# Two small transposes and a run of zero matmuls change places ahead of the first weight group

## Chip, cores, metric

One core of a Trainium2 chip. By the record the rounds of e1 to e4 ran on chip 0, those of e5 to e8 on chip 4 and those of e9 to e12 on chip 12, so a run is compared with the kernel before of its own rounds. Times are device microseconds (us) of that core; lower is better. A span in the trace counts from the first recorded instruction and is some 1.9 us shorter than the reported time.

## The reference, cut to what matters

```python
# [cut: inputs; x is 2048 x 576, weights 576 x 4608, all bf16]
xn = layernorm(x)
return x + ssm(xn, Lambda_re, Lambda_im, log_dt, ...) + glu(xn, w_gate, w_up, w_down)

def glu(x, w_gate, w_up, w_down):
    return (sigmoid(x @ w_gate) * (x @ w_up)) @ w_down
```

The gated part dominates on TensorE. The state-space part needs three rows of 576 constants (log_dt, Lambda_re, Lambda_im), spread over partitions.

## The kernel before

At the start, x tiles of 128 rows are normalised, transposed on TensorE into a PSUM tile, and copied to SBUF by ACT and DVE. Two x tiles make the first 256 columns of xT, which the first weight group multiplies. The three constant rows are loaded as 27 rows of 64 (`crows`) and turned by two small transposes, written into a spare tenth block of the *second* x tile's PSUM tile.

```python
def consts_transpose(ps):                       # two transposes, 27 x 64 each
    for half in (slice(0, H), slice(H, P)):
        nc.tensor.transpose(ps[half, 0:3 * NH], crows[:], ident[0:3 * NH, 0:3 * NH])

def busy(n, cols):                              # zero matmuls: nobody reads the result
    for i in range(n):
        nc.tensor.matmul(start_groups[0].ps[:, i % 2, 0:cols], warm[:, 0:P], warm[:, 0:cols], ...)

ptrs = [psum.tile([P, NH + 1, P], BF16, ...) for _ in range(2)]   # NH = 9 blocks and a spare
busy(10, TB)                                    # at the very start, while x is loaded
busy(6, P)
# [cut]
for tt in range(2):
    ln_recip(0, tt, tt + 1)
    ln_norm(tt, twice=False)
    start_transpose(tt)                         # 18 transposes into ptrs[tt]
consts_transpose(ptrs[1][:, NH, :])             # the spare block of the SECOND x tile
busy(18, P)
start_copy(0, slice(0, NH), nc.scalar.copy)     # ACT: all 9 blocks of the first x tile
ln_stats(2)
start_copy(1, slice(0, 5), nc.scalar.copy)      # ACT: blocks 0 to 4 of the second
# [cut]
start_copy(1, slice(5, NH), nc.vector.tensor_copy)   # DVE: blocks 5 to 8 of the second
for tt in range(2, TT_B):
    ln_recip(0, tt, tt + 1)
    ln_norm(tt, twice=False)
start_groups[0].mms(slice(0, 2 * P))            # the first weight group (L501)
start_transpose(2)
start_transpose(3)
start_groups[1].mms(slice(0, 2 * P))            # the second weight group
# [cut]
consts_copy(ptrs[1][:, NH, :])                  # DVE reads the constants, some 4 us later
```

The kernel states no waits: the framework sets semaphores from what each instruction reads and writes. GpSimd loads the weights, one transfer of 288 KB for each half (gate on partitions 0 to 63, up on 64 to 127).

Of the kernel before, what the change touches and what calls it, by code (L numbers as in the profile page):

```python
# [66 lines left out]
def kernel(  # L67
# [18 lines left out]
    P = 128  # L86
# [107 lines left out]
    def consts_transpose(ps):  # L194
        for half in (slice(0, H), slice(H, P)):
            nc.tensor.transpose(ps[half, 0:3 * NH], crows[:], ident[0:3 * NH, 0:3 * NH])  # L196
# [40 lines left out]
    def ln_recip(nb, t0, t1):  # L237
        nc.vector.reciprocal(rstds[nb][:, t0:t1], rstds[nb][:, t0:t1])
# [4 lines left out]
    def ln_norm(tt, twice=True):  # L243

        nb, tl = divmod(tt, TT_B)
        m, r = mvs[nb][:, tl, 0:1], rstds[nb][:, tl:tl + 1]
        if twice:
            xn = xn_bufs[ln_count[0] % XN_BUFS]
            ln_count[0] += 1
            nc.vector.tensor_scalar(xn[:], halves2(xts[tt][:]), m, r, ALU.subtract, ALU.mult)  # L250
            xns[tt] = xn[:, :, 0, :]
            xn2[tt] = xn
        else:
            xn = hpool.tile([P, NH, H], BF16, name="xn0", tag="hst", bufs=10)
            nc.vector.tensor_scalar(xn[:], xts[tt][:].rearrange("p (c h) -> p c h", h=H), m, r,
                                    ALU.subtract, ALU.mult)
            xns[tt] = xn[:]
# [479 lines left out]
    def busy(n, cols):  # L737
        for i in range(n):
            nc.tensor.matmul(start_groups[0].ps[:, i % 2, 0:cols], warm[:, 0:P], warm[:, 0:cols], start=True, stop=True)  # L739
# [4 lines left out]
    def start_transpose(tt):  # L744
        for c in range(NH):
            for half in (slice(0, H), slice(H, P)):
                nc.tensor.transpose(ptrs[tt % 2][half, c, :], xns[tt][:, c, :], ident[:])  # L747

    def start_copy(tt, cs, eng):
        eng(xT_tile(0)[:, cs, tt * P:(tt + 1) * P], ptrs[tt % 2][:, cs, :])  # L750
# [4 lines left out]
    for tt in range(2):  # L755
        ln_recip(0, tt, tt + 1)
        ln_norm(tt, twice=False)
        start_transpose(tt)
    consts_transpose(ptrs[1][:, NH, :])
    busy(18, P)  # L760
    start_copy(0, slice(0, NH), nc.scalar.copy)
    ln_stats(2)
    start_copy(1, slice(0, 5), nc.scalar.copy)
# [128 lines left out]
```

## Time and profile before

| kernel before | value |
|---|---|
| time, 3 runs | 507.41 us median (507.36 to 507.81) |
| profiled run | 507.63 us, span 505.7 |
| TensorE busy | 500.9 us (99%) |
| last of the three constants' rows, issue to landing | 2.41 to 7.66 |
| first weight group starts | 9.04 |
| second weight group starts | 11.25 |

A timeline row gives start, duration, engine, source line, operation, output and inputs, and a count where equal rows are merged; in brackets stands how long the engine was idle before it and what ended that. PE is TensorE, PEld its weight load, ACT is ScalarE, DVE is VectorE and POOL is GpSimd; xT is the transposed x, pgu a group's output in PSUM. L196 are the constants' transposes, L739 the zero matmuls, L747 the x transposes, L750 the copies out of PSUM, L501 a weight group, L255 the normalisation of an x tile. Where I give a landing or a signal, it is from the trace's semaphore records, which hold the time of every increment. Lines that do not bear on the point are left out of the views without a mark.

### The profile page before, as it was taken

Reading aid. Unit: us, or ns where it says so; the run is one execution under the profiler, and the core shown is the slowest. Engines: PE = TensorE matmul, PEld = TensorE weight load, DVE = VectorE, ACT = ScalarE, POOL = GpSimd, SP = SyncE. Lnnn points to the kernel's source line nnn. Section 1 sums busy time; section 2 is a strip of 40 time slices with the busy share of each in tenths; the row PEclk is TensorE's granted clock in tenths of the full one; section 3 lists DMA queues with packets and bytes.
Section 4 is the critical chain, followed back from the end, with each engine's and each line's share of the span. In section 5 each row is a group of like instructions: output and inputs, shape, how many; then the busy total and the mean of one; then the engine's idle time right before and its main releaser. Section 6 shows DMA issues by size and latency. Waiting matters only on the chain.

```text
span 505.7 us, 10662 instructions
## 1 busy us (share of the span) xinstructions
PE 500.9 (99%) x4536; PEld 289.6 (57%) x4536; DVE 324.6 (64%) x706; ACT 204.8 (40%) x368; POOL 90.8 (18%) x134
## 2 busy tenths in 40 slices
PE   8999999999999999999999999999999999999997
PEld 5544675444477444467764444774444774446775
DVE  5889797887888687878687768786675222222111
ACT  4955733556500756530016655005655005553000
POOL 7216320123100043110001231100431001300000
PEclk9999999999999999999999999999999999999999
DMA  8997595055220096241340652200643201600101
GB/s 207 205 183 232 134 204 89 19 147 141 49 49 25 1 180 152 68 119 58 83 95 6 160 141 49 47 25 1 162 106 86 48 25 27 184 1 1 36 25 35
DMA packets 40949, 45.59 MB, mean 90 GB/s; under 512 B 28614, under 2 KB 32326, under 8 KB 40902
## 3 DMA queue, kind: packets, MB, share of 16 engines
q0 software_dynamic: 10608, 34.22, 28.1%
q1 hardware_dynamic: 29862, 10.37, 10.6%
q8 instruction: 35, 0.57, 0.5%
q10 hardware_dynamic: 432, 0.33, 0.2%
q14 instruction: 12, 0.10, 0.1%
HBM read 34.36 MB, written 2.36 MB: 73 GB/s over the span
## 4 chain that ended last, share of the span: by engine, by line
PE 98%; DMA 1%; SPq 0%; issue 0%; DVE 0%
PE pgu L501 55%; PE pd L575 34%; PE pbu L530 7%; DMA crows<-in_A_Lambda_im_dram 1%; PE pd L583 1%; PE ptr L747 0%; PE pgu L739 0%; SPq L139 0%; SPq L192 0%; DVE ob L584 0%; PE ptr L196 0%
## 5 line engine op out<-in xcount | busy, mean ns | idle before, releaser
L501 PE MATMUL pgu<-xT,wgu 64*128 64x512 bf16 (+1 forms) x2628 | 283.7, 373 | 0.0
L501 PEld LDWEIGHTS <-wgu 64*128 64x128 bf16 x2628 | 127.7, 94 | 150.9 <-issue 0.5
L575 PE MATMUL pd<-wd,hT 128*128 128x288 bf16 x1128 | 141.4, 286 | 0.0
L507 ACT ACTIVATE sT<-pgu 128x512 bf16<-128x512 f32 x144 | 86.4, 600 | 120.8 <-PE pgu L501 119.8
L575 PEld LDWEIGHTS <-hT 128*128 128x128 bf16 x1128 | 109.9, 98 | 30.1 <-DVE hT L510 0.8
L510 DVE TENSOR_TENSOR hT<-sT,uT 128x512 bf16<-128x512 bf16 x144 | 60.6, 421 | 94.8 <-ACT uT L508 94.5
L508 ACT CAST uT<-pgu 128x512 bf16<-128x512 f32 x144 | 84.0, 583 | 0.0
L154 POOL DMA_DIRECT2D wgu<-in_B_w_gate_dram x36 | 27.6, 766 | 234.9 <-PE pgu L501 222.8
L536 ACT COPY bure<-pbu 128x512 f32<-128x512 f32 x16 | 9.4, 585 | 88.8 <-PE pbu L530 75.0
L160 POOL DMA_DIRECT2D wd<-in_B_w_down_dram x36 | 26.3, 734 | 98.6 <-PE pd L575 98.5
L595 DVE TENSOR_TENSOR acc<-acc,pd 128x576 f32<-128x576 f32 x32 | 24.0, 750 | 27.7 <-PE pd L575 27.7
L592 DVE TENSOR_TENSOR ob<-acc,pd 128x576 bf16<-128x576 f32 x15 | 11.3, 754 | 40.9 <-PE pd L575 40.9
L530 PE MATMUL pbu<-xT,bt 64*128 64x512 bf16 x288 | 33.7, 376 | 0.0
L575 PEld LDWEIGHTS <-hst 128*128 128x128 bf16 x270 | 26.4, 98 | 6.7
L154 POOL DMA_DIRECT2D wgu<-in_B_w_up_dram x36 | 26.5, 736 | 1.9 <-DMA wgu<-in_B_w_up_dram 1.9
L445 DVE TENSOR_TENSOR_SCAN gre<-r,g0re,wrim 128x512 bf16<-128x512 f32 x20 | 25.6, 1278 | 0.1
L575 PE MATMUL pd<-ctre,hst 128*128 128x288 bf16 x120 | 24.6, 286 | 0.0
L575 PE MATMUL pd<-ctim,hst 128*128 128x288 bf16 x120 | 24.6, 286 | 0.0
L530 PEld LDWEIGHTS <-bt 64*128 64x128 bf16 x288 | 13.8, 94 | 17.1 <-issue 0.7
L452 DVE TENSOR_TENSOR_SCAN gim<-r,g0im,wrim 128x512 bf16<-128x512 f32 x16 | 20.4, 1274 | 0.0
L230 DVE BATCH_NORM_STATS2 bnst<-xt 128x6 f32<-128x288 bf16 x32 | 12.5, 432 | 2.3 <-DMA xt<-in_A_x_dram 2.2
L431 DVE TENSOR_TENSOR wrim<-T,bure 128x512 bf16<-128x512 bf16 x20 | 13.7, 684 | 0.0
(119 smaller groups left out, 279.6 us busy)
## 6 DMA issues: line engine op xcount, KB each, us to landing
wgu<-in_B_w_gate_dram POOLq DMA_DIRECT2D x36, 288.0 KB, 4.2
wgu<-in_B_w_up_dram POOLq DMA_DIRECT2D x36, 288.0 KB, 4.8
wd<-in_B_w_down_dram POOLq DMA_DIRECT2D x36, 288.0 KB, 5.6
out_dram<-ob SPq DMA_DIRECT2D x15, 144.0 KB, 1.8
xt<-in_A_x_dram SPq DMA_DIRECT2D x10, 144.0 KB, 2.7
xt<-in_A_x_dram POOLq DMA_DIRECT2D x4, 144.0 KB, 7.5
bt<-ctre POOLq DMA_DIRECT2D x2, 288.0 KB, 6.4
bt<-ctim POOLq DMA_DIRECT2D x2, 288.0 KB, 7.8
```

Source lines behind the costliest of these rows:

```text
L154: eng.dma_start(w[rows, :, :], src[:, fs].rearrange("(c p) f -> p c f", p=H))
L160: nc.gpsimd.dma_start(wd[:], B_w_down[f0:f0 + FP * P, :].rearrange("(n p) d -> p n d", p=P))
L431: nc.vector.tensor_mul(w, t1, a[:])
L445: nc.vector.tensor_tensor_scan(gre[:], r_bc, w[:, 0, :], g0re[:, col], ALU.mult, ALU.add)
L452: nc.vector.tensor_tensor_scan(gim[:], r_bc, w[:, 1, :], g0im[:, col], ALU.mult, ALU.add)
L501: nc.tensor.matmul(self.ps[:, gi, cols], w[rows, c, fs], xT[self.nb][rows, c, cols], start=c == 0, stop=c == NH - 1)
L507: nc.scalar.activation(sT[:], self.ps[:, 0, :], ACT.Sigmoid)
L508: nc.scalar.copy(uT[:], self.ps[:, 1, :])
L510: nc.vector.tensor_mul(h[:], sT[:], uT[:])
L530: nc.tensor.matmul(out, w, xT[self.nb][rows, c, ts_], start=c == 0, stop=c == NH - 1)
L575: nc.tensor.matmul(out, lhsT, rhs[:, a * DH:(a + 1) * DH], start=i == 0, stop=i == n - 1)
L595: nc.vector.tensor_add(halves(acc[:]), halves(acc[:]), pd[:, :, 0:DH])
```

## The change

Its intent: TensorE stood still until the constants' rows had landed. With the zero matmuls first, the rows have time to land behind them; and since TensorE then waits less, 14 zeros are to do where 18 stood.

```diff
         ln_norm(tt, twice=False)
         start_transpose(tt)
+    busy(14, P)
     consts_transpose(ptrs[1][:, NH, :])
-    busy(18, P)
     start_copy(0, slice(0, NH), nc.scalar.copy)
```

## The prediction

> **What bounds the kernel now.** I first read the page's engine shares and its chain of work that ended last, to see whether anything but TensorE sets the time.
>
> ```profile
> PE 500.9 (99%) x4536; PEld 289.6 (57%) x4536; DVE 324.6 (64%) x706; ACT 204.8 (40%) x368; POOL 90.8 (18%) x134
> PE 98%; DMA 1%; SPq 0%; issue 0%; DVE 0%
> ```
>
> TensorE is the bound from the first real weight group to the end; DMA is 1% of the chain. So whatever moves the start of that group (L501) moves the end by as much, and nothing else at the start counts. Next I read the chain in order of time over the first 60 us:
>
> ```profile
> 2.41 5.25 DMA crows<-in_A_Lambda_im_dram
> 7.66 0.14 issue
> 7.79 0.20 PE ptr L196 x2
> 7.99 1.11 PE pgu L739 x18
> 9.11 1.09 PE pgu L501 x18
> 10.19 1.13 PE ptr L747 x36
> 11.32 45.79 PE pgu L501 x450
> ```
>
> The constants' rows (crows) land at 7.66; only then can their two transposes (L196) run, then 18 zero matmuls (L739), then the first weight group. TensorE had finished the transposes of the second x tile by about 7.03: the timeline of that stretch starts the last of them at 6.97, and they are spaced 0.056 a pair. It therefore stands idle from 7.03 to 7.76, behind a transfer whose result is not needed until 12.52 (the casts to cvals). That wait is what the change aims at. Then I read the timeline between 6 and 9.3 us, all engines, for what else the first group needs:
>
> ```profile
> 6.70 1.12 ACT L750 COPY xT<-ptr 128x1152 bf16<-128x1152 bf16 x1 [0.95 <-PE ptr L747]
> 7.76 0.14 PEld L196 LDWEIGHTS <-crows 27*64 27x64 bf16 x2 [0.73 <-issue]
> 7.79 0.20 PE L196 MATMUL ptr<-ident,crows 27*64 27x27 bf16 x2 [0.60 <-DMA crows<-in_A_Lambda_im_dram]
> 7.92 1.01 PEld L739 LDWEIGHTS <-warm 128*128 128x128 bf16 x18
> 8.03 0.69 ACT L750 COPY xT<-ptr 128x640 bf16<-128x640 bf16 x1 [0.22 <-PE ptr L196]
> 8.76 0.42 DVE L750 COPY xT<-ptr 128x512 bf16<-128x512 bf16 x1 [0.41 <-ACT xT L750]
> 9.04 1.16 PE L501 MATMUL pgu<-xT,wgu 64*128 64x256 bf16 x18
> ```
>
> The line to dwell on is the ACT copy at 8.03. It moves the first five column blocks of the second x tile out of PSUM, and the first weight group reads them. ACT ended its earlier copy at 7.82, and the x transposes were long done, but it waited 0.22 more for L196: the constants are written into the same PSUM tile as that x tile. The semaphore records agree: TensorE's completion count moves at 6.67 (first x tile) and next at 8.01 (constants), never at the end of the second x tile. The copy signals at 8.73, so it is already done when the first group starts at 9.04. The second half of the weights, one transfer of 288 KB issued at 2.33, lands at 8.46 by its semaphore.
>
> **What the Trainium skill says.** "PSUM — Partial Sum Buffer", under the bank collisions, asks that accesses be guarded by bank and quadrant. A block here is 256 bytes and a bank is 2 KiB by that page, so blocks 0 to 4 lie in the tile's first bank and the constants, in block 9, in its second: the copy need not wait. The trace shows that this program's dependency is coarser; it waits. "TensorEngine Tiling (Array Packing)", Key Properties, says a change of tiling mode drains TensorE. The trace agrees: where 64-row groups give way to transposes, nine pairs of 0.109 from 9.04 end at 10.02, yet the next row starts at 10.12, so a switch costs about 0.09. "TensorE: Matmul & The Clock Gate", in "What's actually happening", says the array halves its clock after an idle window of about 3.4 us. The zero matmuls are there for that: the first ten took 0.43 each for 512 columns, those at 7.93 are spaced 0.056 for 128. No run here shows how long an idle is too long, but the present 0.73 did not slow the matmuls after it.
>
> **The change, part by part.** *Moved:* 14 zero matmuls now stand directly behind the second x tile, where nothing holds them. They start at 7.03 + 0.09 (switch) = 7.12, and take about 14 x 0.056 + 0.01 = 0.80, to 7.92. The old wait for the transfer is thereby covered: crows landed at 7.66. *Removed:* four zero matmuls, 4 x 0.056 = 0.22. *The constants* come after a switch, weight load at 7.92 + 0.10 = 8.02, matmul 0.03 later at 8.05. In the kernel before, the completion count moved 0.21 after the second matmul started (7.80 to 8.01), so now at 8.26, against 8.01.
>
> Taken alone, TensorE's own stream would reach the weight group at about 8.05 + 0.13 = 8.18, or 0.86 earlier than 9.04. But the group needs two more things. Weights: landed at 8.46, plus the 0.10 that crows took from landing to weight load, 8.56. Copy: it still waits for the constants, now behind the zeros, so it starts at 8.26 + 0.02 = 8.28, signals 0.70 later (8.03 to 8.73 before) at 8.98, and TensorE sees it some 0.04 later (the x tile signalled at 5.92 was loaded at 5.96): **9.02**. The maximum is 9.02, against 9.04. The saving is about 0.02 us: the visible wait is removed and comes back as an idle of some 0.8 us between the constants and the first group.
>
> Behind that: the DVE copy of the remaining blocks and the normalisation of x tiles 2 and 3 move with the ACT copy, 0.25 later. Block 5 is read 0.55 into the group, at 9.57; its DVE copy, which signalled at 9.19, signals at about 9.44. Tile 2 is signalled at 9.98 against a reading at 10.10; tile 3 at 10.51 (10.26 before), plus 0.04, against a reading at 10.58 (10.60 before). All just hold, the last by 0.03, so at worst a few hundredths are lost. Nothing later changes in order or amount. Sum: 507.41 - 0.02 = 507.39, which I call **507.4 us**.
>
> **The rivals.** *The full gain.* If TensorE's wait were all that counted, the group would start at 8.18 and the time be 506.55. Against it: the weights' landing at 8.46, which alone cuts the gain to 0.48 (506.9), and the copy. *The copy is not tied to the constants* in the new order and waits for the x transposes only: it would start at 7.85, signal at 8.55, and the group start at 8.59, giving 506.96. For it: the bytes and banks are disjoint. Against it: exactly this copy, with the same bytes, waited for L196 in the trace, and the new program still issues the constants ahead of it. *The clock.* The idle moves to directly ahead of real matmuls, and lasts from about 8.1 to 9.0. If it halved the clock for one idle window, 3.4 us of matmuls would take 3.4 more by the skill's figure, an estimate: 510.8. Against it: the 0.73 idle left spacing at 0.056, and idle time is hardly longer in sum. *The transfer's chance.* The landing of crows at 7.66 is one sample. The kernel before follows it one to one (group 1.38 behind it); the new one is free of it until 7.92. A landing at 8.0 would make the change gain about 0.25, one at 7.3 would make it lose some 0.3, since the zeros before then end earlier.
>
> **Range and chances.** The start of the group can move by -0.5 to +0.4 through these; run to run the time before already spans 507.36 to 507.81, 0.45. I give 506.8 to 508.0. Two per cent is 10.1 us; the whole stretch ahead of the first weight group is only 9.0 us, of which the change touches 2. A gain of 2% is practically excluded, and a loss of 2% needs something of which the profile shows no sign: same 0.98, and 0.01 on either side.
>
> **What would show it.** Right: the zeros start near 7.1 with no idle for crows; L196 near 8.05; the ACT copy near 8.3 with L196 still its releaser, after an idle of about 0.45; the first L501 matmul near 9.0, waiting for that ACT copy; 0.056 spacing kept. Wrong: the copy starting near 7.85 (then the group near 8.6, held by weights), a first group spaced 0.2 instead of 0.109 a pair (clock), TensorE waiting for the normalised tile 3 near 10.6, or crows or weights landing at quite other times. If TensorE's idle ahead of L501 is gone and the time has still not fallen, my chain is wrong.

## The result, and the profile after

| | before | after |
|---|---|---|
| same rounds, 6 runs each, median | 507.38 us (507.01 to 507.81) | 507.72 us (507.56 to 507.95) |
| ratio | | 1.0007 (95% interval 0.9994 to 1.002) |
| profiled run | 507.63 | 507.77 |

A ratio is the mean time of one kernel's fast runs over the mean of the other's of the same rounds, so it isn't quite the ratio of the medians. By the 2% rule the two are the same, and this interval holds 1. The later rounds repeated it (second experiment): over all, 11 runs of the changed kernel have a mean of 507.76, 38 of the kernel before 507.42. That is about 0.34 slower, where the standard error of each mean, worked out from the spread of these runs, is 0.05. The ranges differ too: 507.52 to 507.99 against 506.90 to 508.31, so it is the kernel before that varies.

The chain of work that ended last, in order of time, of the changed kernel (start, length, what):

```profile
6.15 1.23 PE ptr L747 x36
7.38 0.89 PE pgu L739 x14
8.27 0.15 PE ptr L196 x2
8.42 0.02 issue
8.44 0.70 ACT xT L750
9.14 0.04 issue
9.18 1.16 PE pgu L501 x18
11.47 45.79 PE pgu L501 x450
```

The transfer of the rows is gone from the chain; x transposes, zeros and constants run through; and in its place stands an ACT copy of 0.70 between the constants and the first weight group. The timeline of the same stretch shows who waits:

```profile
7.31 0.96 PE L739 MATMUL pgu<-warm 128*128 128x128 bf16 x14
8.20 0.20 PE L196 MATMUL ptr<-ident,crows 27*64 27x27 bf16 x2
8.32 0.09 PEld L501 LDWEIGHTS <-wgu 64*128 64x128 bf16 x1
8.44 0.69 ACT L750 COPY xT<-ptr 128x640 bf16<-128x640 bf16 x1 [0.44 <-PE ptr L196]
9.18 1.16 PE L501 MATMUL pgu<-xT,wgu 64*128 64x256 bf16 x18 [0.79 <-ACT xT L750]
```

TensorE's 0.60 of idle ahead of L196 has become 0.79 ahead of L501, and ACT's idle has grown from 0.22 to 0.44. The gate half's weights are loaded at 8.32; the matmul on them waits for the copy.

One check says that nothing behind this stretch plays a part. The reported time of the profiled run less the start of the second weight group is 507.63 - 11.25 = 496.38 before and 507.77 - 11.40 = 496.37 after, and 496.35 to 496.37 in ten of the twelve profiles below (all but the two of late rows). **The time is decided before the second weight group starts.** An executed run's time can therefore be read as a start of that group.

### The profile page after: what moved, and what is told of

It reads as the page before. It is cut to its first block, busy times and chain, and to the rows that moved or that the text cites. A ratio compares the mean times of both kernels' runs of the same rounds, so it can differ in the third digit from the quotient of the medians.

```text
span 505.9 us, 10654 instructions
## 1 busy us (share of the span) xinstructions
PE 500.5 (99%) x4532; PEld 289.4 (57%) x4532; DVE 325.0 (64%) x706; ACT 204.8 (40%) x368; POOL 91.3 (18%) x134
## 3 DMA queue, kind: packets, MB, share of 16 engines
HBM read 34.36 MB, written 2.36 MB: 73 GB/s over the span
## 4 chain that ended last, share of the span: by engine, by line
PE 98%; DMA 1%; DVE 1%; ACT 0%; issue 0%
PE pgu L501 55%; PE pd L575 34%; PE pbu L530 7%; PE pd L583 1%; DMA xt<-in_A_x_dram 1%; PE ptr L747 0%; DVE bnst L230 0%; PE pgu L739 0%; ACT xT L750 0%; DVE xn L255 0%; DVE mv L231 0%; DVE ob L584 0%; PE ptr L196 0%; DVE rstd L238 0%
## 5 line engine op out<-in xcount | busy, mean ns | idle before, releaser
L501 PE MATMUL pgu<-xT,wgu 64*128 64x512 bf16 (+1 forms) x2628 | 283.7, 373 | 0.8 <-ACT xT L750 0.8
L501 PEld LDWEIGHTS <-wgu 64*128 64x128 bf16 x2628 | 127.8, 94 | 151.5 <-DMA wgu<-in_B_w_up_dram 0.8
```

What stands on the lines that cost most here:

```text
L501: nc.tensor.matmul(self.ps[:, gi, cols], w[rows, c, fs], xT[self.nb][rows, c, cols], start=c == 0, stop=c == NH - 1)
```

## The experiments

The theory: behind the x transposes three things race, and the first weight group starts when the last of them is there: TensorE's own stream, the weights, and the ACT copies. The new order puts the zeros ahead of the constants and thereby, through the shared PSUM tile, ahead of the copy. Rivals: the difference is chance; the weights or x hold the group; the clock drops in the new idle; the number of zeros matters, not their place.

All runs were timed in 5 rounds. "To the group" is the distance from the start of the second x tile's last transpose to the start of the first weight group, which takes the arrival of x out of the comparison. The landing is that of the last constants' row.

| kernel | rows land | last x transpose | group | to the group | median us (range) | ratio to before |
|---|---|---|---|---|---|---|
| before, first profile | 7.66 | 6.97 | 9.04 | 2.07 | 507.41 (507.36 to 507.81) | |
| e1 before again | 6.29 | 6.97 | 8.45 | 1.48 | 507.13 (507.02 to 507.87) | 0.9997 |
| after, first profile | 6.70 | 7.16 | 9.18 | 2.02 | 507.72 (507.56 to 507.95) | 1.0007 |
| e2 after again | 6.20 | 7.17 | 9.19 | 2.02 | 507.89 (507.52 to 507.99) | 1.0008 |
| e3 other tile | 6.51 | 6.94 | 8.43 | 1.49 | 507.17 (506.99 to 507.29) | 0.9995 |
| e12 other tile again | 6.94 | 7.14 | 8.66 | 1.52 | 507.44 (507.25 to 507.52) | 0.9997 |
| e4 behind the group | 7.12 | 7.16 | 8.65 | 1.49 | 507.44 (507.19 to 507.59) | 0.9999 |
| e5 fourteen only | 6.71 | 7.00 | 8.49 | 1.49 | 507.25 (507.08 to 507.45) | 0.9998 |
| e6 moved only | 7.18 | 7.12 | 9.37 | 2.25 | 507.96 (507.77 to 508.39) | 1.0012 |
| e7 rows early, x late | 4.44 | 7.00 | 8.49 | 1.49 | 508.60 (508.25 to 508.76) | 1.0023 |
| e8 other tile, no zeros | 5.83 | 7.11 | 8.60 | 1.49 | 507.43 (507.28 to 507.73) | 1.0003 |
| e9 before, rows late | 8.74 | 7.46 | 10.12 | 2.65 | 509.62 (509.28 to 509.69) | 1.0039 |
| e10 after, rows late | 9.17 | 7.40 | 10.28 | 2.89 | 509.59 (509.05 to 509.76) | 1.0038 |
| e11 rows early, x kept | 5.66 | 7.12 | 8.60 | 1.49 | 507.33 (507.30 to 507.37) | 0.9995 |

The kernel before had, in the rounds of e1 to e4, a median of 507.35; of e5 to e8, 507.36; of e9 to e12, 507.53 (nine runs each). The 95% intervals of e7, e9 and e10 lie above 1; all others hold 1 (e6 just: 0.9999 to 1.0026), and by the 2% rule every run is the same as the kernel before. So what follows rests on the profiles, one for each run, and less on the times.

### e1: the kernel before, again

No edit.

> The kernel before, unchanged, against itself: how far one profile can be trusted. Main theory: the first weight group starts about 1.38 us after the constants' rows land, or at the earliest about 2.1 us after the second x tile is normalised (copy at once, 0.70 for it, weights by then landed), whichever is later. In the first profile the rows landed at 7.66 and the group started at 9.04. Expected: ratio 1.000 within 0.001, and a group start that moves with the rows' landing if that differs by some tenths. Rival (something else sets the start): the start stays near 9.04, or moves, without regard to the landing.

Measured: ratio 0.9997, and the rows landed at 6.29. The chain of this profile:

```profile
5.96 1.23 PE ptr L747 x36
7.19 0.13 PE ptr L196 x2
7.32 1.11 PE pgu L739 x18
8.43 0.03 issue
8.45 1.16 PE pgu L501 x18
```

The transfer isn't in the chain. The constants follow the x transposes without idle, and the group starts at 8.45, not 9.04. The ACT copies follow each other without a wait (x2):

```profile
6.69 1.71 ACT L750 COPY xT<-ptr 128x1152 bf16<-128x1152 bf16 x2 [0.95 <-PE ptr L747]
```

They end at 8.40, within some hundredths of the zeros, which the chain names; which of the two holds the group is told by e5. So **the wait that the first profile showed is not usually there.** In the ten profiles in which the rows were loaded in the original place of the program they landed between 5.83 and 7.66, and only once clearly behind the end of the x transposes: in the profile from which I predicted. The group started 1.48 behind the last x transpose; my "2.1 from the normalisation" (6.45) was 2.0.

### e2: the changed kernel, again

No edit.

> The changed kernel, unchanged. Main theory: its first weight group starts 2.54 to 2.58 us after the second x tile is normalised (zero matmuls 0.8, switch, constants, ACT copy 0.70), whatever the landing of the constants' rows, as long as they land before the zero matmuls end. Expected: that distance within 0.05, and a time 0.0 to 0.5 us above the kernel before (ratio 1.0000 to 1.0010). Rival (the difference of the medians is noise of the start): the ratio falls below 1.0000 as often as above.

Measured: 507.89, ratio 1.0008, group again 2.02 behind the last x transpose although the rows were 0.5 earlier. Counted from the normalisation, as I had put it, the distance was 2.85 and not 2.54 to 2.58: a miss of form. In this execution the zeros at the very start held the x transposes up (the last of them began at 6.03, the first x tile was normalised at 5.81), because the array reached its full clock late: the last six zeros were still 0.107 apart, against 0.056 in the first profile of either kernel. Counted from the transposes the distance holds.

The time is also longer by something new: the second weight group began 2.36 behind the first, against 2.22 in the first profile. The timeline of DVE and GpSimd:

```profile
9.49 0.74 POOL L154 DMA_DIRECT2D wgu<-in_B_w_gate_dram  x1 [0.56 <-DMA wgu<-in_B_w_gate_dram]
9.70 0.63 DVE L255 TENSOR_SCALAR xn<-xt,mv,rstd 128x576 bf16<-128x576 bf16 x1
10.39 0.67 PEld L747 LDWEIGHTS <-xn 128*64 128x64 bf16 x22 [0.32 <-DVE xn L255]
```

The normalisation of the third x tile took 0.63 instead of 0.43, and its transposes waited for it. In the first profile it ran free at 9.69 and took 0.43. The last section comes back to this.

### e3: the constants in the other PSUM tile

```diff
     busy(14, P)
-    consts_transpose(ptrs[1][:, NH, :])
     start_copy(0, slice(0, NH), nc.scalar.copy)
+    consts_transpose(ptrs[0][:, NH, :])
...
-    consts_copy(ptrs[1][:, NH, :])
+    consts_copy(ptrs[0][:, NH, :])
```

The order on TensorE is that of the changed kernel. The spare block is now that of the *first* x tile, whose copy stands ahead in the program, so the second x tile's copy shares no tile with the constants. The coupling is turned round: now the constants have to wait for the first tile's copy. Here the zeros hide that; in e8, without them, it shows.

> The changed kernel, same order on TensorE, but the constants are transposed into the spare block of the first x tile's PSUM tile, whose copy is placed ahead in the program, so that the ACT copy of the second x tile no longer shares a tile with them. Main theory (the copy's wait for the constants is the wait that took the old one's place): the ACT copy starts directly after the earlier copy, about 0.4 us earlier than in the changed kernel, and the first weight group starts when the second half of its weights has landed plus 0.1, near 8.6 to 8.7: 0.4 to 0.5 us earlier than in the changed kernel, so 507.2 to 507.3, ratio to the kernel before 0.9990 to 1.0000. Rival (the weights or TensorE's own stream hold the group, the copy's wait only fills the same time): no change, group near 9.1.

Measured: 507.17 against 507.89 for the changed kernel in the same rounds. From the timeline:

```profile
6.66 1.71 ACT L750 COPY xT<-ptr 128x1152 bf16<-128x1152 bf16 x2 [0.95 <-PE ptr L747]
7.09 0.95 PE L739 MATMUL pgu<-warm 128*128 128x128 bf16 x14
7.97 0.20 PE L196 MATMUL ptr<-ident,crows 27*64 27x27 bf16 x2
8.43 1.16 PE L501 MATMUL pgu<-xT,wgu 64*128 64x256 bf16 x18 [0.25 <-ACT xT L750]
```

Both ACT copies now run back to back (x2, no wait between), while zeros and constants pass beside them. The group starts 1.49 behind the last x transpose, 0.53 earlier than in the changed kernel. One thing was altered, the tile that holds the constants, and the lost time went. **The copy's wait for the constants is what took the old wait's place.** The rival, that weights or TensorE's stream fill the same time, fell. What holds the group here is the pair of copies: 6.66 + 1.71, and 0.06 to TensorE. I had expected the weights to hold it; they had landed at 7.85.

### e4: the constants behind the first group

```diff
     busy(14, P)
-    consts_transpose(ptrs[1][:, NH, :])
...
     start_groups[0].mms(slice(0, 2 * P))
+    consts_transpose(ptrs[1][:, NH, :])
     start_transpose(2)
```

> The constants' transposes behind the first weight group instead of ahead of it; 14 zero matmuls ahead of the group. Main theory: neither TensorE nor the copy waits for the constants, the group starts at 8.6 to 8.7 as in the run with the constants in the other tile, and the constants cost their own 0.1 to 0.2 later, on the path: 507.2 to 507.4 in all, ratio 0.9990 to 1.0002. Rival (only TensorE's order counts, as the change intended): group at 8.02, held by nothing, 506.7 or less.

Measured: the group 1.49 behind the transposes, as in e3, so the rival (8.02) fell; the copies hold it. But the second group follows 2.42 behind the first instead of 2.22: the constants now cost their own 0.13 on the path, and the next normalisation ran into a weight issue again (0.69). Time 507.44, just above what I expected and no better than before.

### e5: only the number of zeros

```diff
     consts_transpose(ptrs[1][:, NH, :])
-    busy(18, P)
+    busy(14, P)
```

> The kernel before with 14 zero matmuls instead of 18, the constants still ahead of them: the removal alone. Main theory: when the rows land early (6.2 to 7.1, as in the later profiles) the group waits for the ACT copies, not for the zeros, so four zeros fewer save nothing: group near 8.45 to 8.65; when the rows land at 7.7 it saves 0.22. Expected time 507.0 to 507.5, ratio to the kernel before 0.9993 to 1.0003. Rival (the zeros' length sets the start, so the change's loss comes from elsewhere): 0.22 us less in every run, group near 8.2.

Measured: 507.25; group 1.49 behind the transposes, as with 18 zeros in e1. Four zeros fewer saved nothing there, because with early rows the copies end last. The rival (0.22 saved) fell. In this profile the up half's weights landed at 8.58, and the group's second matmul waited for them until 8.63, so the weights are close behind the copies.

### e6: only the place

```diff
-    busy(14, P)
+    busy(18, P)
     consts_transpose(ptrs[1][:, NH, :])
```

> The changed kernel with 18 zero matmuls instead of 14: the move alone. Main theory: every zero matmul ahead of the constants delays the constants, the copy and the group by its 0.056: group 0.22 later than in the changed kernel, near 9.4, distance from the second x tile's last transpose 2.25 instead of 2.02; time 507.9 to 508.2, ratio to the kernel before 1.0010 to 1.0016. Rival (the group waits for weights or x, the zeros are hidden): same as the changed kernel, 507.7.

Measured: 507.96, ratio 1.0012, distance 2.25: the 0.22 above the changed kernel are four zeros of 0.056. Each zero ahead of the constants is paid in full. So the two halves of the change are told apart: the move costs, and the four zeros left out give part of that back.

### e7: the rows early, at the cost of an x tile

```diff
     for tt in range(TT_B):
         load_x(tt, nc.sync if tt % 2 == 0 else nc.scalar)
+        if tt == 0:
+            for i, src in enumerate((A_log_dt, A_Lambda_re, A_Lambda_im)):
+                nc.sync.dma_start(crows[i * NH:(i + 1) * NH, :], src.rearrange("(a p) -> a p", p=H))
```

and the same loop taken out of its old place.

> The kernel before with the constants' rows loaded right behind the first x tile on the same queue, ahead of the third. Main theory: the spread of the kernel before is the landing of these rows; here they always land ahead of the second x tile's transposes, so the group starts at 8.4 to 8.7 with only the arrival of x to vary: 507.0 to 507.3, never above 507.5, ratio 0.9988 to 0.9998. Rival (the spread has another source): same median and spread as the kernel before, 506.9 to 507.9.

A miss: 508.60. The group did start 1.49 behind the transposes, but the third x tile, issued behind the rows at 2.29, landed at 7.84 instead of 4.2, and that blocked DVE, as the chain shows:

```profile
2.29 5.56 DMA xt<-in_A_x_dram
7.84 0.02 issue
7.87 0.83 DVE bnst L230 x2
```

I had moved one late transfer into another's place. It tells nothing on the rows; e11 repeats it without this fault.

### e8: e3 without the 14 zeros

```diff
-    busy(14, P)
     start_copy(0, slice(0, NH), nc.scalar.copy)
     consts_transpose(ptrs[0][:, NH, :])
```

> The constants in the first x tile's PSUM tile as in the third experiment, and no zero matmul between the x transposes and the first group (those at the very start stay). TensorE then idles about 1.3 us there. Main theory (nothing but the ACT copies sets the group, the zeros only fill): group at 8.4 to 8.7, pairs still spaced 0.109, 507.0 to 507.3. Rival (the clock rival of the prediction: the zeros keep the array's clock up): pairs spaced 0.2 in the first group and those after it, time above 508.

Measured: distance 1.49 as with the zeros, and 507.43, 0.1 above what I expected. TensorE did nothing from about 7.17 to 8.60 but two small transposes, which waited until 8.00 for the first tile's copy, and the pairs of the first groups were still about 0.109 apart: no sign of a lower clock. In the profiled execution (507.40) the excess is the weights: the up half landed at 8.79, the group's second matmul waited for it, and the second group came 2.45 behind the first instead of 2.22. The other four executions were not traced.

```profile
8.60 1.39 PE L501 MATMUL pgu<-xT,wgu 64*128 64x256 bf16 x18 [0.40 <-ACT xT L750]
8.83 0.87 PEld L501 LDWEIGHTS <-wgu 64*128 64x128 bf16 x17 [0.61 <-DMA wgu<-in_B_w_up_dram]
```

So the clock rival fell for idles of this length (0.8 and 0.5, with the transposes between), and the zeros in this place did nothing for the clock that this trace shows.

### e9 and e10: both kernels with late rows

In both, the three row loads are issued on GpSimd's queue behind the first weights:

```diff
     load_wgu((0, 0), nc.gpsimd, nc.gpsimd)
+    for i, src in enumerate((A_log_dt, A_Lambda_re, A_Lambda_im)):
+        nc.gpsimd.dma_start(crows[i * NH:(i + 1) * NH, :], src.rearrange("(a p) -> a p", p=H))
```

and taken out of their old place.

> The kernel before, its constants' rows loaded on GpSimd's queue behind the first weights, so that they land after the x transposes in every run, probably between 8 and 11 us. Main theory: the group starts 1.38 us after the landing (0.10 to the weight load, 0.16 for the constants, 18 zeros 1.01, a switch 0.09) and the time is that start plus 498.6, so 508 to 511. Rival (the landing doesn't carry the start): time near 507.4.

> The changed kernel with the same late rows. Main theory: the zeros are over by then, and the group starts 1.08 to 1.13 us after the landing (0.10, constants to ACT copy 0.24, copy 0.70, 0.04), so for the same landing 0.25 to 0.30 us ahead of the kernel before with late rows: here the change pays, ratio of the two means 0.9994 to 0.9995. Rival (the change costs the same whatever the rows do): 0.3 to 0.4 us above the kernel before with late rows.

Measured: landings at 8.74 and 9.17. In the kernel before, the group started 1.38 behind the landing, in the changed one 1.11, both as expected: with late rows the change gains 0.27 at this point. The chain of the changed kernel:

```profile
4.12 5.04 DMA crows<-in_A_Lambda_im_dram
9.30 0.21 PE ptr L196 x2
9.54 0.70 ACT xT L750
10.69 0.08 DVE rstd L238
10.80 0.57 DVE xn L255
```

The times do not show it cleanly: means of 509.49 and 509.57, 0.08 apart in the right direction where I expected 0.25 to 0.30. Two reasons are visible. The landing differed between the executions (0.43 in the two profiles), and in the changed kernel the x transposes then waited for the normalisation, as the end of this chain shows, so the second group came 2.49 behind the first against 2.31. Both kernels also lost some 0.6 to 0.8 later on, perhaps since the loads behind the rows on GpSimd's queue were shifted; I did not follow that. The step at the first group is shown, its worth in time is left open.

### e11: the rows early, the x tiles kept

As e7, and the third x tile goes to ACT's queue ahead of the fourth:

```diff
-        load_x(tt, nc.sync if tt % 2 == 0 else nc.scalar)
+        load_x(tt, nc.sync if tt == 0 else nc.scalar)
```

> The kernel before with the rows loaded right behind the first x tile as in the seventh experiment, but the third x tile moved to ACT's queue, ahead of the fourth, so that it isn't delayed as it was there. Main theory: rows always ahead of the transposes' end, group at 8.4 to 8.7, time 507.0 to 507.4 with none above 507.6. Rival (the spread has another source, such as x or the weights): same median and spread as the kernel before.

Measured: 507.30 to 507.37 in five runs, where the kernel before went from 507.11 to 508.31 in nine runs of the same rounds; median 507.33 against 507.53. Rows at 5.66, distance 1.49. The spread is smaller with early rows, as expected. That the rows are its cause is not shown: five runs are few, and two x tiles were moved along with the rows (the fourth landed at 7.28 instead of 4.35). e3 and e12, which do not wait for late rows either, still spread over about 0.3 each.

### e12: e3 once more

No edit to e3.

> The kernel of the third experiment once more, against the kernel before: the version that should not depend on the rows' landing and has no wait of the copy for the constants. Main theory: 507.0 to 507.3, 0.1 to 0.4 below the kernel before. Rival (the third run's 507.17 was luck): 507.4.

A miss in the time: 507.44 against 507.53, which is the rival's number. The distance held (1.52). In the profiled execution (507.25) the zeros at the very start again ran late, as in e2, and the x transposes began 0.27 behind the first tile's normalisation instead of 0.06; that accounts for most of the 0.26 to the profile of e3. Over both, ten runs have a mean of 507.27 against 507.43 and 507.57 of the kernel before in the same rounds. Of the arrangements tried it is the one in which neither the rows' landing (up to some 7.9) nor the constants delay either group. In the means it beats the kernel before by 0.16 and 0.30 in the two sets of rounds, and the changed kernel by 0.5. Against the kernel before, neither interval excludes equality (0.9982 to 1.0007, 0.9984 to 1.0011).

## Why the prediction was right or wrong

The range held (507.72 in 506.8 to 508.0) and the class was right, but neither was hard: the range also held two of the prediction's own rivals (506.9 and 506.96), and no kernel tried here moved the time by even 0.5%. The sign was missed: 0.02 less was forecast, about 0.34 more was measured. By its own steps:

- *TensorE bounds everything, so only the start of the first group counts:* right. Time less the second group's start is the same to 0.03 in twelve profiles.
- *Zeros in 0.80, switch 0.09, constants, signal 0.21 later, copy 0.70, TensorE 0.04:* right to 0.04 in each term. Predicted distance from the last x transpose 9.02 - 6.97 = 2.05, measured 2.02, twice.
- *The copy stays tied to the constants; an idle of 0.8 takes the old one's place:* right, 0.79 by the profile, and e3 shows the cause.
- *The full gain (506.55), the untied copy (506.96), the clock (510.8):* all fell, the first by e4, the second by the profile after, the third by that profile too (pairs 0.109 apart behind the idle) and by e8. The sum of the third was also too large: at half the clock for one window of the 3.4 that the prediction cites, half of that time is lost, an estimate of 1.7 and not 3.4.
- *Weights landed plus 0.10, 8.56, before the group can start:* wrong, but hidden under the larger term. Only the group's second matmul needs the up half: in e8 the group started at 8.60 and the half landed at 8.79.
- *"Group at 9.02, against 9.04":* **here the sum was mis-sized.** The term was the start of the group in the kernel before, 9.04, taken from one execution with the rows at 7.66. With early rows it is 1.48 to 1.49 behind the x transposes instead of 2.07 (e1, and e5 with 14 zeros), because the copies then end last; so the change then costs 2.02 - 1.49 = 0.53 instead of saving 0.02. The means differ by 0.34, between the two cases. I had named the rows' landing as a rival and put the loss at "some 0.3" for a landing at 7.3, but had centred the number on the late landing.
- *Tile 3's normalisation just holds, by 0.03:* too tight. In e2 the transposes waited for tile 2, because a normalisation can take 0.63 instead of 0.43.

## What to carry to other kernels

A wait in one profile is a sample: where a small transfer ends it, look at several executions before building on its length. When an instruction is moved past a wait, follow everything that is ordered behind it, including what shares only a tile with it; here one result nobody needed for 4 us held back a copy that everything needed. Filler work belongs behind the instruction that others wait for, not ahead of it: in e6 each zero ahead of the constants cost its 0.056.

## What the Trainium skill lacked or had wrong

- "SBUF — State Buffer", Who interferes with whom, says that DVE and GpSimd share a port pair and that, where a DVE instruction in one of its two-port modes meets a GpSimd one, whoever issues first has the pair and the other blocks. It gives no size for a case like this. In the profiles here a normalisation that started 0.15 to 0.32 after GpSimd began to issue a weight load took 0.57 to 0.70 instead of 0.43 (10 of 10 cases); and each ended 0.11 to 0.14 after the issue did; one that started 0.03 to 0.14 after it kept 0.43, and then the issue took 0.77 to 0.88 instead of some 0.73 (5 cases). That is the kind of blocking which the page describes, but not the whole of it: issues of x tiles that began 0.26 before a normalisation left it at 0.43 (e2). No run took the issue away, so the cause isn't shown.
- "DMA: Bandwidth & Descriptors", Latency and other measured facts, gives about 0.8 us as the least for a tiny transfer and about 2 us as the fixed cost of one. Three loads of 1.1 KB beside the weights' loads took 3.4 to 5.3 from the last issue (2.40 to 2.45) to the last landing (5.83 to 7.66 in ten profiles). The page has no figure for such a tail.
- No page has it: that a program's own tracking of who waits for whom may be coarser than the guard by bank and quadrant which the prediction names. Here it held a copy for a write in another bank, and e3 gained 0.53 at the first group by changing the tile alone.
- "TensorE: Matmul & The Clock Gate", PE-mode transpose, gives about 275 ns as the duration of a 128 x 128 transpose in one kernel and says that the full clock doesn't engage in this mode. Here each half-width transpose (64 columns, 128 moving) is recorded with 219 ns, but a pair follows the last every 0.056 us. That is the spacing of the zero matmuls at full clock (0.107 before it), so the full clock was in force here. Whether transposes alone would bring it about no run shows.
